# Attention scores of two head pairs as 64x64 products in four quarters of the array, one low part of g on GpSimd, and another order of the token blocks

## The chip, the cores and the metric

One core of one Trainium2 chip. The metric is the time of one execution on the device, in microseconds (us); a kernel's time is the median of its runs. Lower is better.

## The reference

Windowed attention (4 batches, 8 heads, 576 positions, head size 64, window 64), then a gated layer with a rational function, then a product of two linear layers. Cut to what matters:

```
scores = (q @ k.T) / 8                       # only 0 <= i - j < 64 is kept
attn   = softmax(scores)
x      = (attn @ v)  as  2304 tokens x 512
h = x @ w_in                                 # 512 -> 2048
P = a0 + a1*h + a2*h^2 + a3*h^3
Q = 1 + |b0|*|h| + |b1|*h^2
x = (P / (Q + 1e-6)) @ w_out                 # 2048 -> 512
h = (x @ w1) * (x @ w2) @ w3                 # 512 -> 1024 -> 1024
out = h @ w_out2                             # 1024 -> 512
```

The weights arrive as float64; the kernel rebuilds float32 values from the two 32-bit words and keeps them as a high and a low part, so that a product is three products (line 272, `TERMS`).

## The kernel before, in words

The program is not written in the order in which it runs. Each piece of work is declared to a planner (`Plan`, line 66) with the engines it may run on, a cost on each, what it comes after, the buffers it takes and, for some, a due time; the planner simulates all engines, breaks ties with a seeded random number (line 223) and emits every engine's instructions in the order that it found. The order on TensorE is guided by a hand-made sequence (lines 313 to 380): `AT` says at which pair of chunks each attention step stands, `TS`, `TT`, `TO` are costs of scores, transposes and weighted sums.

**Attention.** The 2304 tokens are cut into five blocks (`TOKENS`, line 30), each into two units; a block of 384 has units of 192 tokens (3 windows of 64), a block of 512 has units of 256 (4 windows). A step is one unit and one pair of heads: 40 steps, which come in 20 pairs (`attn`, line 536). A step loads `q`, `k`, `v` (lines 589 to 606), forms for each window the scores of 64 queries against 128 keys (`S_`, line 609), takes the masked minimum on VectorE (`tr`, line 618), the exponential on ScalarE (`e`, line 624), normalizes (`nm`, line 627, on ScalarE, GpSimd or VectorE as the planner chooses), transposes (`T`), copies back (`ac`) and multiplies with `v` (`O`, line 563). The result of a pair is split into a high part (`xh_`, ScalarE) and a low part (`xl_`, VectorE, line 580). In the blocks of 384 that stand first (`THIN`, 16 steps) the two heads of a step are two 64x64 products per window, one in the upper left and one in the lower right quarter of the array. In the other 24 steps a window is one 128x128 product, with the queries of the two heads laid out block-diagonally and padded with zeros by the host (`queries(u, True)`).

**The gated stage.** `chunks` (line 685) takes two chunks of 128 hidden columns at a time, 40 such chunk pairs: `H_` (line 699) into `hp`, the rational function on ScalarE and VectorE (lines 712 to 775), and `D_` (line 777) into four accumulators. Its last step is the low part of `g` (`lo`, line 773), one instruction per chunk, so 80 in all, on VectorE or GpSimd by the planner's choice (line 818). Half of the chunk pairs use another form of the polynomial (`estrin`, line 697). The first three blocks are walked in halves of the hidden columns (`TURNS`, line 307), so their partial sums are stored and added later (`evacuate`, line 831). Between these the weights are rebuilt and split (`conv`, line 431: b0, b1, b2 and lo on VectorE, hi on ScalarE), 72 tiles, with due times (`coming`, lines 887 to 891).

**The rest** is the product of `w3` and the last weight (`w_prod`, line 939) and a scheme with seven products for the two-sided layers (lines 981 to 1256). The change doesn't touch it.

Of the kernel before, what the change touches and what calls it, by code (L numbers as in the profile page):

```python
# [12 lines left out]
F32 = mybir.dt.float32  # L13
# [16 lines left out]
TOKENS = (384, 384, 512, 512, 512)  # L30
# [7 lines left out]
NU = len(US)  # L38
NF = FF // P
# [26 lines left out]
class Plan:  # L66
# [30 lines left out]
    def order(self, rounds=16):  # L97
# [125 lines left out]
        rng = Random(67)  # L223
# [21 lines left out]
def body(ctx: ExitStack, tc: tile.TileContext, qkv, kv0, qk0, w_in, w_out, a, b, w1, w2, w3t, wo2, out):  # L245
# [72 lines left out]
    MM = [{384: TMM, 512: TWM}[t] for t in TOKENS]  # L318
# [4 lines left out]
    TS, TT, TO, TOO = 0.67, 0.33, (0.71, 0.42), 1.9  # L323
# [11 lines left out]
    def then_step(what, i):  # L335
        if 0 <= i < NS:
            then((what, i), {"S": TS, "T": TT, "O": TO[i % 2]}[what] * WIDE(i))
# [11 lines left out]
    for t in range(-2 * NP - 1, NI + 1):  # L349
        scale[0] = 2.9 / (TS + TT + TO[0]) if t < 0 else 1.2 if t < 2 * NP * 2 else 1.0  # L350
# [185 lines left out]
    def attn(pair):  # L536
# [46 lines left out]
        def step(k):  # L583
# [5 lines left out]
            def load(_):  # L589
                x["k"] = ap_.tile([P, KB * W_], F32, tag="k", bufs=rings["k"], name="k")[:, 0:KU]  # L590
                if i < THIN:
                    if k == 0:
                        y["q"] = ap_.tile([P, 2 * UM], F32, tag="q", bufs=rings["q"], name="q")[:, 0:2 * U]
                        nc.sync.dma_start(out=y["q"], in_=qk0[u, p0 // 2])
                    x["q"] = y["q"].rearrange("d (k w n) -> d k w n", k=2, w=NW)[:, k]
                    nc.sync.dma_start(out=x["k"], in_=kv0[u, p, :, 0:KU])
                    return
                q = ap_.tile([P, 2 * UM], F32, tag="q", bufs=rings["q"], name="q")[:, 0:2 * U]
                x["q"] = q.rearrange("d (w n) -> d w n", w=NW)
                nc.sync.dma_start(out=q, in_=qkv[u - THIN // NP, p, :, 0:2 * U])  # L600
                nc.sync.dma_start(out=x["k"], in_=qkv[u - THIN // NP, p, :, 2 * U:2 * U + KU])

            def loadv(_):
                y["v", k] = ap_.tile([P, NWM, P], F32, tag="v", bufs=rings["v"], name="v")[:, 0:NW]
                v = kv0[u, p, :, U + W_:] if i < THIN else qkv[u - THIN // NP, p, :, 2 * U + KB * W_:]
# [3 lines left out]
            def S_(_):  # L609
                x["sp"] = sp = psum.tile([P, NW, P], F32, tag=tags[0], bufs=rings[tags[0]], name="sp")  # L610
                x["sm"] = ap_.tile([P, NWM, P], F32, tag="sm", bufs=rings["sm"], name="sm")[:, 0:NW]
                if k == 0:
                    y["st"] = ap_.tile([P, 8 * NWM], F32, tag="st", bufs=rings["st"], name="st")
# [38 lines left out]
            kb_, vb, qb, mb, sp, tp = ("k", i), ("v", i), ("q", i0 if i < THIN else i), ("sm", i), (tags[0], ("S", i)), (tags[1], ("T", i))  # L652
            thin = i < THIN
            op(("load", i), (("D", (0.48 if k else 1.12) if thin else 1.1 * wide),), load, after=[("load", i0)] if thin and k else (), new=(kb_,) if thin and k else (kb_, qb), uses=(qb,) if thin and k else (), tail=3.0)
            op(("loadv", i), (("D", 0.66 * wide),), loadv, after=(("load", i),), new=(vb,), tail=3.0)
            pe(("S", i), S_, TS * wide, after=[("load", i)] + [("S", i - 1)] * k, new=(sp, mb) if k else (sp, mb, sb), uses=(kb_, qb, sb) if k else (kb_, qb))
            for m in range(NW):
                op(("tr", i, m), (("V", 0.21),), lambda _, m=m: tr(m), after=(("S", i),), uses=(sp, mb, sb))
                op(("e", i, m), (("A", 0.39),), lambda _, m=m: e(m), after=(("tr", i, m),), uses=(mb, sb))
            op(("nm", i), (("A", 0.32 * NW), ("P", 0.97 * wide), ("V", cost(0.065, 0.40))), nm, port=True, after=(("rc", i0),), uses=(sb, mb))  # L660
            moved = i >= MOVED
            if moved:
                op(("mv", i), (("D", 0.66 * wide),), mv, after=[("nm", i)], new=(("tq", i),), uses=(mb,), tail=3.0)
            pe(("T", i), T, 0.068 * NW if moved else TT * wide, after=[("mv", i)] if moved else [("nm", i)], new=(tp,), uses=(("tq", i),) if moved else (mb,))
# [20 lines left out]
    def chunks(c0):  # L685
# [205 lines left out]
    coming = {key: 3.2 * min(n, 12) + 8.5 * max(n - 12, 0) for n, key in enumerate(coming)}  # L891
# [391 lines left out]
def layouts(q, k, v, moe_w_in, moe_w_out, moe_a, moe_b, moe2_w1, moe2_w2, moe2_w3, moe2_w_out):  # L1283
# [26 lines left out]
    def queries(u, apart):  # L1310
# [47 lines left out]
```

## Time and profile before

| what | value |
|---|---|
| median of 3 runs | 804.59 us (804.21 to 805.1) |
| the profiled execution | 805.03 us, of which the span from the first to the last instruction 803.3 us |
| mean granted TensorE clock | 0.995 |
| TensorE busy | 782.0 us, 97% |
| VectorE busy | 729.7 us, 91% |
| ScalarE busy | 542.2 us, 67% |
| GpSimd busy | 50.5 us, 6% |
| moved by DMA | 169.70 MB |

The shares are means over stages: start-up (to about 56 us), gated stage (to about 499 us), then the linear layers. Busy time of TensorE is modelled with pipelined ends, so starts of neighbouring groups say more than durations.

### The profile page before, as it was taken

The page shows a single profiled execution, that of the slowest core. Times are in us where ns is not written, and L with a number is a line of the kernel's source. Part 1 is how long each engine was busy: PE and PEld are TensorE (multiplying, and loading weights), DVE is VectorE, ACT ScalarE, POOL GpSimd, SP SyncE. Part 2 cuts the span into 40 slices and gives each one's busy share as a digit, 9 for nine tenths or more (in the row PEclk, how much of TensorE's full clock was granted, in tenths as well). Part 3 has the DMA queues.
Part 4 walks back from the last instruction along what each step waited for, and adds up shares of the span by engine and source line. Part 5 has one row for each costly group of instructions (what it writes and reads, how often), then busy time and mean ns, then how long its engine had stood idle before and what let it go on. Part 6 is the DMA issues. An engine that isn't in the chain of part 4 may idle for free.

```text
span 803.3 us, 13413 instructions
## 1 busy us (share of the span) xinstructions
PE 782.0 (97%) x4728; PEld 716.3 (89%) x4728; DVE 729.7 (91%) x1361; ACT 542.2 (67%) x1131; POOL 50.5 (6%) x67
## 2 busy tenths in 40 slices
PE   5889999999999999999999999999999999999998
PEld 4679999888899999888888888889999999999998
DVE  6999999999999999999999999999998698847854
ACT  5888998859898988665677772377555447445434
POOL 1112112101100101200100000000000000000000
PEclk9899999999999999999999999999999999999999
DMA  8798884511657755537883365968898676136402
GB/s 292 249 334 305 293 278 157 186 54 65 207 185 282 273 191 203 202 133 236 323 282 143 117 221 183 313 249 292 307 305 282 210 283 195 42 133 222 145 1 78
DMA packets 66403, 169.70 MB, mean 211 GB/s; under 512 B 7456, under 2 KB 24864, under 8 KB 66336
## 3 DMA queue, kind: packets, MB, share of 16 engines
q1 hardware_dynamic: 66336, 168.85, 60.5%
q8 instruction: 37, 0.61, 0.3%
q14 instruction: 30, 0.25, 0.1%
HBM read 123.21 MB, written 41.42 MB: 205 GB/s over the span
## 4 chain that ended last, share of the span: by engine, by line
PE 83%; DVE 12%; DMA 2%; ACT 1%; issue 1%; POOL 0%; SPq 0%; POOLq 0%; DVEq 0%; ACTq 0%
PE acc L781 22%; PE hp L703 20%; PE pb L1093 9%; PE pa L1093 6%; PE pc L1093 6%; PE wp L948 5%; PE pb L1220 5%; PE pc L1220 3%; PE pa L1220 3%; PE sp L616 2%; DVE sm L619 2%; DVE wt L456 1%; DVE wt L453 1%; DVE wc L466 1%; PE op L568 1%; DMA cb<-in_b 1%
## 5 line engine op out<-in xcount | busy, mean ns | idle before, releaser
L703 PE MATMUL hp<-x,wc 128*128 128x512 f32 (+1 forms) x960 | 213.8, 371 | 3.6 <-DVE u L731 3.2
L781 PE MATMUL acc<-g,wc 128*128 128x512 f32 (+1 forms) x960 | 213.1, 370 | 0.0
L703 PEld LDWEIGHTS hp<-x,wc 128*128 128x128 f32 x960 | 173.7, 188 | 27.8 <-DVE u L731 4.2
L781 PEld LDWEIGHTS acc<-g,wc 128*128 128x128 f32 x960 | 173.9, 188 | 22.9 <-issue 0.3
L1093 PE MATMUL pb<-xb,wc 128*128 128x384 f32 x432 | 83.8, 334 | 0.0
L1093 PEld LDWEIGHTS pb<-xb,wc 128*128 128x128 f32 x432 | 75.7, 188 | 0.0
L744 ACT ACTIVATE r<-qa,cq 128x1024 f32<-128x1024 f32 (+1 forms) x40 | 42.8, 1069 | 37.8 <-DVE g L775 21.3
L625 ACT ACTIVATE sm<-sm,st 128x128 f32<-128x128 f32 x144 | 56.1, 395 | 17.3 <-DVE st L619 17.1
L720 ACT ACTIVATE qa<-hp,cb 128x512 f32<-128x512 f32 (+1 forms) x80 | 51.7, 647 | 19.3 <-PE hp L703 19.0
L725 ACT ACTIVATE u<-hp,ca 128x512 f32<-128x512 f32 (+1 forms) x80 | 59.5, 745 | 1.7 <-PE hp L703 1.3
L1093 PE MATMUL pa<-xb,wc 128*128 128x384 f32 x288 | 57.2, 335 | 0.0
L1182 ACT ACTIVATE rt<-prod 128x768 fp32r<-128x768 f32 x42 | 35.6, 847 | 31.9 <-PE pb L1220 13.3
L1093 PE MATMUL pc<-xb,wc 128*128 128x384 f32 x288 | 56.7, 334 | 0.0
L1185 DVE TENSOR_TENSOR rt<-prod,rt 128x768 fp32r<-128x768 f32 x42 | 40.1, 956 | 15.4 <-ACT rt L1182 14.9
L616 PE MATMUL sp<-k,q 64*64 64x128 f32 (+1 forms) x384 | 43.2, 311 | 10.2 <-DMA k<-in_kv 7.2
L463 ACT ACTIVATE wc<-wt 128x512 fp32r<-128x512 f32 x48 | 30.2, 633 | 32.7 <-DVE wt L456 29.0
L1093 PEld LDWEIGHTS pa<-xb,wc 128*128 128x128 f32 x288 | 50.6, 188 | 0.3 <-DMA wc<-kw 0.2
L453 DVE SCALAR_TENSOR_TENSOR wt<-ws,wt 128x512 uint32<-128x512 uint32 x72 | 50.4, 702 | 0.3
L1093 PEld LDWEIGHTS pc<-xb,wc 128*128 128x128 f32 x288 | 50.5, 188 | 0.0
L456 DVE SCALAR_TENSOR_TENSOR wt<-ws,wt 128x512 uint32<-128x512 uint32 x72 | 49.9, 695 | 0.3
L616 PEld LDWEIGHTS sp<-k,q 64*64 64x64 f32 (+1 forms) x384 | 37.9, 182 | 13.7 <-DMA k<-in_kv 4.0
L715 ACT ACTIVATE h<-hp 128x512 f32<-128x512 f32 (+1 forms) x80 | 44.3, 553 | 8.2 <-PE hp L703 7.1
(90 smaller groups left out, 1368.4 us busy)
## 6 DMA issues: line engine op xcount, KB each, us to landing
wc<-kw SPq DMA_DIRECT2D x48, 512.0 KB, 5.4
bs<-kb SPq DMA_DIRECT2D x24, 512.0 KB, 4.5
ws<-in_w_in SPq DMA_DIRECT2D x16, 512.0 KB, 6.1
ws<-in_w_out SPq DMA_DIRECT2D x16, 512.0 KB, 4.2
ws<-in_w SPq DMA_DIRECT2D x16, 512.0 KB, 4.3
kw<-ws SPq DMA_DIRECT2D x16, 512.0 KB, 3.5
ws<-in_w3t SPq DMA_DIRECT2D x16, 512.0 KB, 4.8
wsum<-wsum SPq DMA_DIRECT2D x16, 512.0 KB, 6.1
```

The lines of the kernel that those rows point to most:

```text
L453: stt(out=x["b"], in0=x["st"][:, :, 0], scalar=29, in1=x["b"], op0=ALU.logical_shift_right, op1=ALU.bitwise_or)
L456: stt(out=x["b"], in0=x["st"][:, :, 1], scalar=0xC0000000, in1=x["b"], op0=ALU.bitwise_and, op1=ALU.bitwise_or)
L616: nc.tensor.matmul(sp[h, w, :], x["q"][h, w], x["k"][h, kat[w] * W_:kat[w] * W_ + P], start=True, stop=True)
L625: act(x["sm"][:, m, :], x["sm"][:, m, :], AF.Exp, bias=col(0, k, m), scale=-1.0, accum_out=col(1, k, m))
L703: nc.tensor.matmul(x["hp", m], wf_(win, f0 + m)[:, s_, kk * P:(kk + 1) * P], (xh, xl)[m_][xk][:, kk, :], start=(kk == 0 and i == 0), stop= ...
L715: act(x["h2"][:, m, :], x["hp", m], AF.Square)
L720: act(x["qa"][:, m, :], x["hp", m], AF.Abs, scale=b0)
L725: act(x["u"][:, m, :], x["hp", m], AF.Identity, scale=a3, bias=a2)
L744: act(x["r"], x["qa"], AF.Ln, bias=cq)
L781: nc.tensor.matmul(accs[j, part, n], wf_(wout, f0 + m)[:, s_, n * P:(n + 1) * P], x["g"][:, m_, m, :], start=(first and i == 0), stop=(las ...
L1093: nc.tensor.matmul(x[m], sws[u, n, i0][:, s_, (c0 + k) * P:(c0 + k + 1) * P], t[:, m_, k, :], start=(first and k == 0 and i == 0), stop=(k ...
L1220: nc.tensor.matmul(x[m, n], w[:, s_, (c + n) * P:(c + n + 1) * P], rts[u, b, r][:, m_, k, :], start=(first and r == 0 and k == 0 and i == ...
```

## The change

- **Scores.** All blocks now use 64x64 products. `S_` exists once per pair of steps and issues, for each window, four products: both heads of the first step in the upper left and lower right quarter, both heads of the second step in the other two quarters. The second step's heads thus change places in its score tile, and `O` reads them back from there. The padded queries are gone; one load of `q` serves two steps in all blocks. The scores of a pair now come after both loads of `k`.
- **Low part of g.** In chunk pairs that are not `estrin`, the second chunk's `lo` may run on GpSimd only. `nm` may no longer run on GpSimd.
- **Order.** `TOKENS` is (384, 512, 384, 512, 512), so the second block is now a wide one; `AT`, the seed, costs and the due times of the weights change with it.

```diff
-TOKENS = (384, 384, 512, 512, 512)
+TOKENS = (384, 512, 384, 512, 512)
...
-        rng = Random(67)
+        rng = Random(50)
...
-        AT[((-8, -6, -4, -2), (0, 1, 2, 3), (4, 5, 6, 6), (16, 18, 19, 20), (22, 24, 25, 26))[j][r // 2]].append(i)
+        AT[((-8, -6, -4, -2), (0, 1, 2, 2), (4, 5, 6, 6), (16, 18, 19, 20), (21, 23, 25, 26))[j][r // 2]].append(i)
...
-                for h in (slice(0, 64), slice(64, P)):
-                    nc.tensor.matmul(y["op"][h, k, w * W_:(w + 1) * W_], y["v", k][:, w, h], y["ac", k][:, w, h], start=True, stop=True)
+                for h in range(2):
+                    at = half[h if k == 0 else 1 - h]
+                    nc.tensor.matmul(y["op"][half[h], k, w * W_:(w + 1) * W_], y["v", k][:, w, half[h]], y["ac", k][:, w, at], start=True, stop=True)
...
+        def S_(_):
+            for k in range(2):
+                y["place", k]()
+            y["st"] = ap_.tile([P, 8 * NWM], F32, tag="st", bufs=rings["st"], name="st")
+            for w in range(NW):
+                for k in range(2):
+                    for h in range(2):
+                        to = half[h if k == 0 else 1 - h]
+                        nc.tensor.matmul(y["sp", k][to, w, :], y["q", k][half[h], w], y["k", k][half[h], kat[w] * W_:kat[w] * W_ + P], start=True, stop=True)
...
-                for w in range(NW):
-                    for h in (slice(0, 64), slice(64, P)) if i < THIN else (slice(0, P),):
-                        nc.tensor.matmul(sp[h, w, :], x["q"][h, w], x["k"][h, kat[w] * W_:kat[w] * W_ + P], start=True, stop=True)
...
-            op(("nm", i), (("A", 0.32 * NW), ("P", 0.97 * wide), ("V", cost(0.065, 0.40))), nm, port=True, after=(("rc", i0),), uses=(sb, mb))
+            op(("nm", i), (("A", 0.32 * NW), ("V", cost(0.065, 0.40))), nm, port=True, after=(("rc", i0),), uses=(sb, mb))
...
+            if not estrin and m == 1:
+                engines = (("P", 0.97 * T_ / 384),)
...
-    coming = {key: 3.2 * min(n, 12) + 8.5 * max(n - 12, 0) for n, key in enumerate(coming)}
+    coming = {key: 3.2 * min(n, 10) + 8.5 * max(n - 10, 0) for n, key in enumerate(coming)}
```

Two places in the order of the instructions. On TensorE, the scores of the first wide block (`sp`, line 616 before and 584 now) among the products of the gated stage (`hp` and `acc`), in the kernel before:

```order
L616 MATMUL sp<-k,q 128x128 x8
L781 MATMUL acc_817<-g,wc 128x384 x3
L781 MATMUL acc_808<-g,wc 128x384 x3
L781 MATMUL acc_771<-g,wc 128x384 x3
L703 MATMUL hp<-x,wc 128x384 x12
L781 MATMUL acc_823<-g,wc 128x384 x3
```

and now, where the wide block is the second one and its scores begin ahead of the first `hp`:

```order
L584 MATMUL sp<-k,q 64x128 x16
L649 MATMUL tp<-idr,sm 128x128 x6
L711 MATMUL hp<-x,wc 128x384 x6
L572 MATMUL op<-sm,v 64x64 x12
L711 MATMUL hp<-x,wc 128x384 x15
L649 MATMUL tp<-idr,sm 128x128 x8
L711 MATMUL hp<-x,wc 128x384 x3
L584 MATMUL sp<-k,q 64x128 x16
```

A wide pair of steps was 8 products of the whole array and is 16 products of a quarter; the first wide pair stood behind the `op` of the second block and now stands ahead of the first `hp`.

On GpSimd, the low parts of `g` (line 775 before, 783 now) about the first chunk pairs of 512 tokens, in the kernel before, with the sums' reciprocal preparation (line 558) and normalizations (line 633) among them:

```order
L775 TENSOR_TENSOR g<-u,r 128x384 x2
L558 TENSOR_SCALAR st<-st 128x8
L633 TENSOR_TENSOR sm<-sm,st 128x512
L558 TENSOR_SCALAR st<-st 128x8
L775 TENSOR_TENSOR g<-u,r 128x384 x3
L558 TENSOR_SCALAR st<-st 128x8
L633 TENSOR_TENSOR sm<-sm,st 128x512
L775 TENSOR_TENSOR g<-u,r 128x512 x3
```

and now, from the first chunk pair of 512 tokens on:

```order
L783 TENSOR_TENSOR g<-u,r 128x512
L561 TENSOR_SCALAR st<-st 128x6
L783 TENSOR_TENSOR g<-u,r 128x512 x2
L561 TENSOR_SCALAR st<-st 128x6
L783 TENSOR_TENSOR g<-u,r 128x512 x2
L561 TENSOR_SCALAR st<-st 128x8
L783 TENSOR_TENSOR g<-u,r 128x512
L783 TENSOR_TENSOR g<-u,r 128x384 x5
```

Over the whole list GpSimd has 28 low parts before (17 of 384 columns, 11 of 512) and 33 now (13 and 20), and 7 normalizations before and none now.

## Rows read from the trace of the kernel before

**Rows 1.** The page, busy time of the engines, share of the span and instructions.
```profile
PE 782.0 (97%) x4728; PEld 716.3 (89%) x4728; DVE 729.7 (91%) x1361; ACT 542.2 (67%) x1131; POOL 50.5 (6%) x67
```

**Rows 2.** Busy time in four stretches: PE, PEld, DVE, ACT, POOL (instructions), clock, DMA share, GB/s.
```profile
0.00:56.00 56.00, 38.82 (x397) 31.82 (x397) 48.30 (x151) 41.90 (x133) 9.15 (x24) 0.94 0.86 290
56.00:487.20 431.20, 430.60 (x2602) 381.10 (x2601) 425.59 (x770) 342.10 (x723) 41.32 (x43) 1.00 0.59 207
...
560.00:803.30 243.30, 239.80 (x1383) 239.27 (x1381) 185.03 (x312) 120.09 (x208) 0.00 (x0) 1.00 0.54 185
```

**Rows 3.** TensorE's waits, 0 to 56 us: total, times, longest.
```profile
PE sp L616 <- DMA k<-in_kv: 7.2, 2, 3.6
PE hp L703 <- DVE u L731: 2.6, 1, 2.6
```

**Rows 4.** TensorE's waits, 56 us to the end, all of them.
```profile
PE hp L703 <- DVE u L731: 0.6, 1, 0.6
```

**Rows 5.** VectorE's waits, 56 to 487 us, the longest.
```profile
DVE st L561 <- POOL st L558: 1.2, 1, 1.2
DVE u L728 <- ACT u L725: 0.9, 1, 0.9
```

**Rows 6.** The chain of waits where the gated stage ends.
```profile
488.47 5.44 PE wp L948 x24
493.91 5.44 PE acc L781 x24
```

**Rows 7.** TensorE in order of time: start, duration, what; a group overlaps the next.
```profile
50.88 1.62 PE L568 MATMUL op<-sm,v 128*64 128x64 f32 x48
52.43 0.79 PE L703 MATMUL hp<-x,wc 128*128 128x384 f32 x3
...
60.28 2.24 PE L703 MATMUL hp<-x,wc 128*128 128x384 f32 x12
62.36 0.68 PE L781 MATMUL acc<-g,wc 128*128 128x384 f32 x3
...
63.46 1.31 PE L781 MATMUL acc<-g,wc 128*128 128x384 f32 x6
64.69 1.53 PE L616 MATMUL sp<-k,q 64*64 64x128 f32 x24
66.15 2.36 PE L781 MATMUL acc<-g,wc 128*128 128x384 f32 x12
...
75.41 1.84 PE L781 MATMUL acc<-g,wc 128*128 128x384 f32 x9
77.08 2.00 PE L616 MATMUL sp<-k,q 128*128 128x128 f32 x16
78.83 1.84 PE L781 MATMUL acc<-g,wc 128*128 128x384 f32 x9
```

**Rows 8.** Groups of VectorE by line and shape: count, busy us, mean ns of one.
```profile
L775 DVE TENSOR_TENSOR g<-u,r 128x512 fp32r<-128x512 f32 x37 | 25.0, 707 | 0.0
...
L775 DVE TENSOR_TENSOR g<-u,r 128x384 fp32r<-128x384 f32 x15 | 8.1, 573 | 0.1
...
L855 DVE TENSOR_TENSOR xe<-xe,acc 128x384 f32<-128x384 f32 x8 | 4.3, 548 | 0.1
...
L855 DVE TENSOR_TENSOR xe<-xe,acc 128x512 f32<-128x512 f32 x4 | 2.6, 680 | 0.0
...
L861 DVE COPY xe<-acc 128x512 f32<-128x512 f32 x1 | 0.7, 695 | 0.0
```

**Rows 9.** The same of ScalarE, the normalization.
```profile
L631 ACT ACTIVATE sm<-sm,st 128x128 f32<-128x128 f32 x69 | 22.1, 393 | 0.7 <-DVE st L561 0.6
```

**Rows 10.** Busy time in one stretch of the start, columns as in group 2.
```profile
40.00:60.00 20.00, 16.07 (x161) 14.16 (x160) 19.64 (x55) 17.62 (x51) 2.33 (x3) 1.00 0.97 337
```

**Rows 11.** All engines in order of time, the first scores.
```profile
7.13 0.43 DVE L450 TENSOR_SCALAR wt<-ws 128x512 uint32<-128x512 uint32 x1 [1.70 <-DMA ws<-in_w_in]
...
8.69 2.82 PE L616 MATMUL sp<-k,q 64*64 64x128 f32 x24 [3.60 <-DMA k<-in_kv]
```

More of the change, by code (lines that the diff above doesn't have):

```diff
@@ L38 @@
 NU = len(US)
+THINU = NU
 NF = FF // P
@@ L244, in body @@
 @with_exitstack
-def body(ctx: ExitStack, tc: tile.TileContext, qkv, kv0, qk0, w_in, w_out, a, b, w1, w2, w3t, wo2, out):
+def body(ctx: ExitStack, tc: tile.TileContext, kv0, qk0, w_in, w_out, a, b, w1, w2, w3t, wo2, out):
     nc = tc.nc
@@ L315, in body @@
         j, r = divmod(i, 2 * NP)
-        AT[((-8, -6, -4, -2), (0, 1, 2, 3), (4, 5, 6, 6), (16, 18, 19, 20), (22, 24, 25, 26))[j][r // 2]].append(i)
+        AT[((-8, -6, -4, -2), (0, 1, 2, 2), (4, 5, 6, 6), (16, 18, 19, 20), (21, 23, 25, 26))[j][r // 2]].append(i)
     TMM, TWM = 0.1735, 0.227
-    MM = [{384: TMM, 512: TWM}[t] for t in TOKENS]
+    MM = [{256: 0.12, 384: TMM, 512: TWM}[t] for t in TOKENS]
     THIN = qk0.shape[0] * NP
@@ L335, in then_step @@
     def then_step(what, i):
-        if 0 <= i < NS:
+        if 0 <= i < NS and (what != "S" or i % 2 == 0):
             then((what, i), {"S": TS, "T": TT, "O": TO[i % 2]}[what] * WIDE(i))
@@ L549, in attn @@
         y = units.setdefault(u, [{} for _ in range(NP // 2)])[p0 // 2]
+        half = (slice(0, 64), slice(64, P))
         def rows(f):
@@ L590, in load @@
                 x["k"] = ap_.tile([P, KB * W_], F32, tag="k", bufs=rings["k"], name="k")[:, 0:KU]
[L591 to L601, printed above, removed]
+                if k == 0:
+                    y["q"] = ap_.tile([P, 2 * UM], F32, tag="q", bufs=rings["q"], name="q")[:, 0:2 * U]
+                    nc.sync.dma_start(out=y["q"].rearrange("d (k n) -> d k n", k=2), in_=qk0[u, p0 // 2].rearrange("d (k n) -> d k n", k=2)[:, :, 0:U])
@@ L603, in loadv, with place @@
+                y["q", k] = y["q"].rearrange("d (k w n) -> d k w n", k=2, w=NW)[:, k]
+                nc.sync.dma_start(out=x["k"], in_=kv0[u, p, :, 0:KU])
+                y["k", k] = x["k"]
             def loadv(_):
                 y["v", k] = ap_.tile([P, NWM, P], F32, tag="v", bufs=rings["v"], name="v")[:, 0:NW]
-                v = kv0[u, p, :, U + W_:] if i < THIN else qkv[u - THIN // NP, p, :, 2 * U + KB * W_:]
+                v = kv0[u, p, :, KU:KU + NW * P]
                 nc.sync.dma_start(out=y["v", k], in_=v.rearrange("r (w d) -> r w d", w=NW))
-            def S_(_):
-                x["sp"] = sp = psum.tile([P, NW, P], F32, tag=tags[0], bufs=rings[tags[0]], name="sp")
+            def place():
+                y["sp", k] = x["sp"] = psum.tile([P, NW, P], F32, tag=tags[0], bufs=rings[tags[0]], name="sp")
@@ L650, in ac @@
                 act(y["ac", k], x["tp"], cp)
-            kb_, vb, qb, mb, sp, tp = ("k", i), ("v", i), ("q", i0 if i < THIN else i), ("sm", i), (tags[0], ("S", i)), (tags[1], ("T", i))
-            thin = i < THIN
-            op(("load", i), (("D", (0.48 if k else 1.12) if thin else 1.1 * wide),), load, after=[("load", i0)] if thin and k else (), new=(kb_,) if thin and k else (kb_, qb), uses=(qb,) if thin and k else (), tail=3.0)
+            kb_, vb, qb, mb, sp, tp = ("k", i), ("v", i), ("q", i0), ("sm", i), (tags[0], ("S", i)), (tags[1], ("T", i))
@@ L655, in step @@
+            thin = True
+            op(("load", i), (("D", (0.48 if k else 1.12) * wide),), load, after=[("load", i0)] if thin and k else (), new=(kb_,) if thin and k else (kb_, qb), uses=(qb,) if thin and k else (), tail=3.0)
             op(("loadv", i), (("D", 0.66 * wide),), loadv, after=(("load", i),), new=(vb,), tail=3.0)
-            pe(("S", i), S_, TS * wide, after=[("load", i)] + [("S", i - 1)] * k, new=(sp, mb) if k else (sp, mb, sb), uses=(kb_, qb, sb) if k else (kb_, qb))
+            if k == 0:
+                sp1, mb1 = (f"acc{(i + 1) % 2}" if early else "at", ("S", i + 1)), ("sm", i + 1)
+                pe(("S", i), S_, TS * wide, after=[("load", i), ("load", i + 1)], new=(sp, mb, sb, sp1, mb1), uses=(kb_, qb, ("k", i + 1)))
@@ L661, in step @@
             moved = i >= MOVED
             if moved:
-                op(("mv", i), (("D", 0.66 * wide),), mv, after=[("nm", i)], new=(("tq", i),), uses=(mb,), tail=3.0)
-            pe(("T", i), T, 0.068 * NW if moved else TT * wide, after=[("mv", i)] if moved else [("nm", i)], new=(tp,), uses=(("tq", i),) if moved else (mb,))
+                op(("mv", i), (("D", 0.66 * wide),), mv, after=[("nm", i)], new=(("tq", i),), uses=(mb,), tail=2.0)
+            pe(("T", i), T, 0.075 * NW if moved else TT * wide, after=[("mv", i)] if moved else [("nm", i)], new=(tp,), uses=(("tq", i),) if moved else (mb,))
@@ L1322, in queries @@
         return out.reshape(NP, P, -1)
-    thin = range(4)
-    qk0 = np.stack([queries(u, False) for u in thin])
+    thin = range(THINU)
+    pad = lambda x: np.concatenate([x, np.zeros((NP, P, KB * W_ + NWM * P - x.shape[2]), x.dtype)], axis=2)
+    qk0 = np.stack([pad(queries(u, False))[:, :, :UM] for u in thin])
     return {
-        "qkv": np.stack([np.concatenate([queries(u, True), keys(u, KB), values(u)], axis=2) for u in range(4, NU)]),
-        "kv0": np.stack([np.concatenate([keys(u, len(blocks(u)[0])), values(u)], axis=2) for u in thin]),
-        "qk0": qk0.reshape(4, NP // 2, 2, P, -1).transpose(0, 1, 3, 2, 4).reshape(4, NP // 2, P, -1),
+        "kv0": np.stack([pad(np.concatenate([keys(u, len(blocks(u)[0])), values(u)], axis=2)) for u in thin]),
+        "qk0": qk0.reshape(THINU, NP // 2, 2, P, -1).transpose(0, 1, 3, 2, 4).reshape(THINU, NP // 2, P, -1),
         "w_in": cols(moe_w_in, NF),
```

9 lines of the change are left out of this document (4 added, 5 removed).

## The prediction

> **What bounds the kernel now.** The page first: TensorE is busy 97% of the span, VectorE 91%, ScalarE 67%, GpSimd 6% [rows 1]. A share over the whole span doesn't say who waits for whom, so the next view is the busy time by stretch [rows 2]. From 56 to 487.2 us, the gated stage with most of the attention in it, TensorE is busy for 430.6 of 431.2 us and VectorE for 425.6: both engines are full at once. From 560 us on TensorE is full and VectorE has 58 us to spare. The list of waits agrees: TensorE's waits lie in the first 56 us, where it is idle for 17.2 us in all [rows 2], 7.2 of it for keys [rows 3]; after that one wait of 0.6 us is all that the list has [rows 4]. So time taken off TensorE in the gated stage is worth its full size only where VectorE can follow, and that is the question of this case. Where the stage ends, TensorE has 5.44 us of the weight product ahead of the last 24 products into the accumulators [rows 6]: work that doesn't need `g` covers the last chain on VectorE.
>
> **Scores.** The timeline shows starts of groups [rows 7]. A wide pair of steps (16 passes over 128 columns of the whole array; float32 takes two passes a product) starts at 77.08 and the next product at 78.83: 1.75 us, 0.109 a pass. The nine products ahead of it take 1.67 us, against 1.56 at the 0.173 of the twelve `hp` that start at 60.28: 0.11 us on entry. Together 1.86. A pair of a block of 384, in two quarters, has 24 passes from 64.69 to 66.15: 1.46 us, 0.061 a pass, so two run at a time (12 x 0.109 = 1.31, and 0.15 at the end). Six products ahead of it take 1.23 us, not 1.04: 0.19 on entry. Together 1.65.
>
> Four at a time is not in the trace; it is bounded by rows. The weighted sums use two column halves over all rows: 48 passes of 64 columns from 50.88 to 52.43, 0.032 each, against half of 0.109: two column halves run at once. The 384 scores show two row halves at once. If both hold together, a 384 pair costs 0.19 + 6 x 0.109 + 0.15 = 0.99 (0.66 less) and a wide pair 0.19 + 8 x 0.109 + 0.15 = 1.21 (0.65 less). If still only two run, a 384 pair stays at 1.65 and a wide pair is 0.19 + 16 x 0.109 + 0.15 = 2.08 (0.22 more). I take four: the pieces that it is made of are both seen, and entry and exit are already paid in the 384 row. The four pairs of the first block lie where TensorE idles anyway, so 16 pairs count: **10.4 us off TensorE** (20 pairs: 13.1).
>
> The two heads of a step write the two partition halves of one PSUM bank, and their 24 passes take half of 24 x 0.109 [rows 7]. The Trainium skill, page "TensorEngine Tiling (Array Packing)", section "Restrictions and Gotchas", says that different row tiles cannot access one PSUM bank at the same time. For halves that differ in partitions the rows here speak against it. By that rule the two heads of a step would exclude each other and at most two products would run: the second bound above, a rival below.
>
> **Low part of g and the rest of VectorE.** In the order of the whole program GpSimd has 33 low parts instead of 28, and they are wider. VectorE has 28 of 512 instead of 37, and 19 of 384 instead of 15: 9 x 0.707 - 4 x 0.573 = 4.1 us less [rows 8]. The other order of blocks makes evacuation dearer: three more copies of accumulators on VectorE (of ScalarE's 19 there are 16 left), one at 0.695 and two that I put at the 0.548 of an addition of that size, and four additions at 0.680 instead of 0.548: 2.3 us more [rows 8]. The normalizations on VectorE stay 14. Sum: **1.8 us less VectorE**. The seven normalizations that leave GpSimd go to ScalarE: 94 windows there instead of 69, 25 x 0.393 = 9.8 us more [rows 9], beside other work on an engine that is busy for 342 of 431 us [rows 2]. I cost it at nothing; if the cover is gone, the exponentials behind it are late, and with them the transposes. GpSimd has the time for five more.
>
> Can VectorE put work off instead? Of 72 weight tiles, 60 have their third conversion step ahead of the fortieth and last update of `qa` (line 764) in the order before, and 60 now. So no: it has the same work up to there, less 1.8 us.
>
> **Order and loads.** The second block now has 32 windows instead of 24, all wanted before the fifth chunk pair; the third has 24 instead of 32. Work moves ahead and none is added. Its loads move ahead too: eight steps with a third more `v` and `q` and longer keys, 1.05 MB by the shapes at the least, where the DMA engines are busy 97% at 337 GB/s [rows 10]. Later loads shrink, since one `q` of 256 KB serves two wide steps (12 loads fewer); no wait in [rows 4] is a DMA, so that is worth nothing. The first scores now wait for both key tiles, until 8.69 instead of 3.55 us [rows 11]; VectorE starts its first conversion at 7.13, and the little that it did before (one masked minimum) it does later: at most 0.4 us, hidden.
>
> **The sum.** From 56 to 487.2 us VectorE idles for 431.2 - 425.6 = 5.6 us [rows 2]; its longest waits there are for GpSimd's sums and ScalarE's `u` [rows 5], not for TensorE directly. With 1.8 us less work the stage can end at most 5.6 + 1.8 = 7.4 us earlier, less than TensorE's 10.4. A faster TensorE feeds ScalarE and through it VectorE, so part of the idle time goes; what waits for ScalarE, which gets 9.8 us more, stays. I take half: 2.8 + 1.8 = 4.6 us. The other 5.8 us of TensorE's gain turn into waits for VectorE. Behind 487 us nothing changes. 805.0 - 4.6 = 800.4 on the profiled execution, which stands 0.4 above the median of the runs: **800.0 us**, with 797.2 (all 7.4) to 802.8 (the 1.8 alone) for this case.
>
> **Rivals.**
> 1. TensorE alone decides. For: it has no waits after 56 us, and the planner may place VectorE's conversions so that none is late. Against: VectorE's 5.6 us of idle time. 804.6 - 10.4 = 794.2, with the first block too 791.5.
> 2. No gain: VectorE's idle time stays, because ScalarE's longer queue holds it, and grows by about as much as the 1.8 us. 803.0 to 806.2, likeliest 804.6.
> 3. The start gets longer. In 20 to 60 us the wide second block's 1.05 MB come on a full DMA; at 300 GB/s that is 3.5 us by which keys, values or weights land later, and VectorE idles. It decides if the loads of weights, whose due times the change also stretches, don't give way. VectorE then has 3.5 us more idle time against 1.8 less work: 804.6 + 1.7 = 806.3, and more if the scores' later start adds to it.
> 4. The change doesn't do what it says: two products at a time only. 12 wide pairs at 0.22 more: 804.6 + 2.6 = 807.2. Against it: the two rows of halves above.
>
> **How the numbers follow.** Forecast 0.50, rival 1 0.21, rival 2 0.15, rival 3 0.08, rival 4 0.06. A measurement of this kernel tells about 0.2% (1.6 us) from no change, so faster is under 803.0: the forecast and rival 1, 0.71. Rival 2 is within: 0.15. Rivals 3 and 4 are above 806.2: 0.14. The range leaves out these two and the lowest end of rival 1: 793.0 to 805.5.
>
> **What would show it.** Right: a wide pair of scores near 1.2 us from start to start; new waits of TensorE for VectorE after 56 us, some 5 us in all; VectorE's idle time up to its fortieth update of `qa` down by about 3 us; the stage's end some 5 us earlier and the rest after it as long as before. Wrong: scores of a wide pair at 2 us (rival 4), TensorE without waits and the end 10 us earlier (rival 1), or TensorE and VectorE idle for loads before 80 us (rival 3).

## The result, and the profile after

The changed kernel takes **811.83 us** (median of 4 runs, 811.58 to 815.98), the kernel before in the same comparison 804.4 us, which is 7.4 us less. The ratio of the means is 1.0103, 95% interval 1.0070 to 1.0137. It is 1% slower; the forecast was 800.0 us, with 793.0 to 805.5 as its range.

The profiled execution spans 810.0 us. Page of the changed kernel, busy time, to be held against [rows 1]:

```profile
PE 776.6 (96%) x4920; PEld 699.6 (86%) x4920; DVE 732.3 (90%) x1359; ACT 545.5 (67%) x1153; POOL 72.0 (9%) x65
```

The same stretches as [rows 2], of the changed kernel:

```profile
0.00:56.00 56.00, 34.33 (x343) 27.18 (x343) 47.36 (x159) 40.47 (x138) 4.10 (x18) 0.91 0.87 289
56.00:487.20 431.20, 423.30 (x2821) 364.69 (x2821) 421.27 (x751) 342.88 (x737) 67.93 (x47) 1.00 0.57 199
```

TensorE now idles 7.9 us in the second stretch, not 0.6, and VectorE 9.9 us, not 5.6. GpSimd is busy for 67.93 us there, not 41.32.

The chain of waits of the changed kernel where the gated stage ends, against [rows 6]:

```profile
497.05 1.21 DVE u L776
498.26 0.68 DVE wt L451 x2
498.93 0.60 DVE wt L454
499.53 0.61 DVE g L783
500.14 0.04 issue
500.19 5.75 PE acc L789 x24
505.94 9.07 PE wp L958 x40
```

The last 24 products into the accumulators end at 505.94 instead of 499.35 us, 6.6 us later, and the span is 6.7 us longer: all of the loss lies in the gated stage, the linear layers after it take as long as before. The chain is VectorE's there; before, it was TensorE's.

For the rest of the text one number stands for the stage: the start of the fortieth and last update of `qa` (line 764 before, 772 after) on VectorE, split into VectorE's busy and idle time ahead of it (the spans of its instructions in the trace, overlaps counted once). Before: 487.1 us = 473.9 busy + 13.2 idle. After: **495.3 = 476.8 + 18.5**. At the 26th update the two kernels stand level, 335.7 and 335.1 us; the loss comes after it.

The scores themselves do what was forecast. TensorE of the changed kernel in order of time, a wide pair twice, against [rows 7]:

```profile
63.28 1.10 PE L584 MATMUL sp<-k,q 64*64 64x128 f32 x32
64.31 1.31 PE L711 MATMUL hp<-x,wc 128*128 128x384 f32 x6
...
69.20 1.10 PE L584 MATMUL sp<-k,q 64*64 64x128 f32 x32
70.23 0.79 PE L789 MATMUL acc<-g,wc 128*128 128x384 f32 x3
```

From start to start it is 1.03 us for 32 passes, where 16 passes of the whole array took 1.75. A pair of a block of 384 takes 0.82 for 1.46:

```profile
99.42 0.89 PE L584 MATMUL sp<-k,q 64*64 64x128 f32 x24
100.24 1.65 PE L711 MATMUL hp<-x,wc 128*128 128x512 f32 x6
```

All scores together take 24.7 us from start to start, 37.9 before. TensorE's busy time on the page falls by 5.4 us only (776.6 for 782.0): the 1152 products of 512 columns in `hp` and `acc` take 5.3 us more by their starts, though their median stays at 0.227 us. What holds single ones up by about 0.1 us is not shown.

What is new is on GpSimd. Its low parts, by line and shape, in the changed kernel:

```profile
L783 POOL TENSOR_TENSOR g<-u,r 128x512 fp32r<-128x512 f32 x20 | 39.1, 1967 | 132.2 <-DVE u L778 53.8 <-DVE u L776 43.7 <-ACT qa L728 16.2
L783 POOL TENSOR_TENSOR g<-u,r 128x384 fp32r<-128x384 f32 x13 | 16.8, 1307 | 67.5 <-DVE u L778 28.2 <-DVE u L776 22.8 <-PE acc L789 8.1
```

and in the kernel before:

```profile
L775 POOL TENSOR_TENSOR g<-u,r 128x384 fp32r<-128x384 f32 x17 | 19.4, 1159 | 65.7 <-DVE u L770 30.9 <-ACT u L725 13.5 <-ACT sm L650 10.8
L775 POOL TENSOR_TENSOR g<-u,r 128x512 fp32r<-128x512 f32 x11 | 14.9, 1370 | 139.4 <-DVE u L768 59.6 <-PE hp L703 41.7 <-DVE u L770 38.0
```

The same instruction over 512 columns takes 1.97 us instead of 1.37 in the mean. Around the longest of them, all engines in order of time (in brackets the idle time before and who ended it):

```profile
409.08 1.27 DVE L748 SCALAR_TENSOR_TENSOR qa<-h,cab,qa 128x1024 f32<-128x1024 f32 x1
409.33 6.59 POOL L783 TENSOR_TENSOR g<-u,r 128x512 fp32r<-128x512 f32 x1 [8.42 <-ACT ws L464]
410.28 0.68 DVE L783 TENSOR_TENSOR g<-u,r 128x512 fp32r<-128x512 f32 x1
410.88 0.68 DVE L467 TENSOR_TENSOR ws<-wt,ws 128x512 fp32r<-128x512 f32 x1
...
411.49 1.21 DVE L758 TENSOR_TENSOR u<-u,h 128x1024 f32<-128x1024 f32 x1
...
412.62 0.41 DVE L451 TENSOR_SCALAR wt<-ws 128x512 uint32<-128x512 uint32 x1
412.96 1.21 DVE L761 TENSOR_TENSOR u<-u,bl 128x1024 f32<-128x1024 f32 x1
414.09 0.68 DVE L454 SCALAR_TENSOR_TENSOR wt<-ws,wt 128x512 uint32<-128x512 uint32 x1
...
415.96 1.15 ACT L752 ACTIVATE r<-qa,cq 128x1024 f32<-128x1024 f32 x1 [6.12 <-POOL g L783]
417.14 1.06 ACT L755 ACTIVATE r<-r 128x1024 f32<-128x1024 f32 x1
...
418.24 1.23 DVE L767 TENSOR_TENSOR g<-u,r 128x1024 fp32r<-128x1024 f32 x1 [3.46 <-ACT r L755]
```

How long a low part takes goes with what VectorE does beside it, not with VectorE being busy. The low part at 409.33 us starts inside a `qa` sum (line 748). That sum and what follows it read two tiles of SBUF, the memory that holds the low part's `u` and `r` too; only line 451, the first step of a conversion, reads one. The last of them ends at 414.77 us, and the low part 1.15 us later. The 61 low parts on GpSimd in the two traces fall in two groups:

- Those that start beside an instruction of VectorE that reads a result of TensorE in PSUM or a single tile of SBUF, or beside none, take 1.00 to 1.02 us at 384 columns and 1.27 to 1.30 at 512, though VectorE is busy nearly all the while: 23 of 28 before, 15 of 33 now.
- Those that start where VectorE is in, or just entering, an instruction with both inputs in SBUF take 1.29 to 2.79 us and once 6.59: 5 of 28 before, **18 of 33** now. Against the short times (1.01 and 1.29) GpSimd's low parts take 17 us more in all, 3 before.

The planner has a rule for this: `ports` (line 93 before, 94 now) never lets a GpSimd operation overlap one of VectorE that is marked `port`. But only the order of its plan is kept on the chip, not the times, and 15 of the 18 start beside a marked one. The other three start beside steps of a conversion (lines 454 and 457) that are not marked.

A low part reads `r`, of which there is one buffer. ScalarE can't write the next `r` until GpSimd is done, and VectorE needs that `r` for the next `g`. ScalarE's waits, 56 us to the fortieth update, changed kernel:

```profile
ACT r L752 <- DVE g L783: 21.3, 9, 4.0
ACT r L752 <- POOL g L783: 13.6, 5, 6.1
```

For GpSimd's low parts (line 775) ScalarE waited 0.8 us, once, in the kernel before. VectorE's longest waits in the same stretch, changed kernel, against [rows 5]:

```profile
DVE g L767 <- ACT r L755: 4.2, 3, 3.5
DVE u L736 <- ACT h L723: 1.5, 3, 0.6
DVE sm L625 <- PE sp L584: 1.4, 4, 0.6
```

And TensorE's, 56 us to the stage's end, against [rows 4]:

```profile
PE acc L789 <- DVE g L783: 2.9, 3, 1.9
PE hp L711 <- DVE u L739: 2.8, 4, 1.3
```

### The profile page after: what moved, and what is told of

Same layout as the page of the kernel before. It is cut to its first block, busy times and chain, and to the rows that moved or that the text cites. A ratio compares the mean times of both kernels' runs of the same rounds, so it can differ in the third digit from the quotient of the medians.

```text
span 810.0 us, 13831 instructions
## 1 busy us (share of the span) xinstructions
PE 776.6 (96%) x4920; PEld 699.6 (86%) x4920; DVE 732.3 (90%) x1359; ACT 545.5 (67%) x1153; POOL 72.0 (9%) x65
## 4 chain that ended last, share of the span: by engine, by line
PE 59%; DVE 28%; ACT 7%; issue 3%; DMA 2%; POOL 0%; SPq 0%; DVEq 0%; ACTq 0%; POOLq 0%
PE acc L789 11%; PE hp L711 10%; PE pb L1103 8%; PE pa L1103 6%; PE pc L1103 6%; PE wp L958 5%; PE pb L1230 5%; PE pc L1230 3%; PE pa L1230 3%; DVE qa L748 3%; DVE qa L772 3%; DVE wt L454 2%; DVE wt L457 2%; DVE g L783 2%; ACT sm L631 2%
## 5 line engine op out<-in xcount | busy, mean ns | idle before, releaser
L783 POOL TENSOR_TENSOR g<-u,r 128x512 fp32r<-128x512 f32 (+1 forms) x33 | 56.0, 1707 | 199.7 <-DVE u L778 82.0
L1103 PE MATMUL pc<-xb,wc 128*128 128x384 f32 x288 | 56.5, 334 | 0.0
L748 DVE SCALAR_TENSOR_TENSOR qa<-h,cab,qa 128x1024 f32<-128x1024 f32 (+1 forms) x40 | 50.1, 1252 | 0.3 <-ACT h L723 0.3
L457 DVE SCALAR_TENSOR_TENSOR wt<-ws,wt 128x512 uint32<-128x512 uint32 x72 | 49.1, 682 | 0.2
L454 DVE SCALAR_TENSOR_TENSOR wt<-ws,wt 128x512 uint32<-128x512 uint32 x72 | 49.0, 682 | 0.2
```

What stands on the lines that cost most here:

```text
L454: stt(out=x["b"], in0=x["st"][:, :, 0], scalar=29, in1=x["b"], op0=ALU.logical_shift_right, op1=ALU.bitwise_or)
L457: stt(out=x["b"], in0=x["st"][:, :, 1], scalar=0xC0000000, in1=x["b"], op0=ALU.bitwise_and, op1=ALU.bitwise_or)
L748: stt(out=x["qa"], in0=x["h2"], scalar=b1, in1=x["qa"], op0=MUL, op1=ADD)
L783: engine[e].tensor_tensor(out=x["g"][:, 1, m], in0=x["u"][:, m], in1=x["r"][:, m], op=MUL)
L1103: nc.tensor.matmul(x[m], sws[u, n, i0][:, s_, (c0 + k) * P:(c0 + k + 1) * P], t[:, m_, k, :], start=(first and k == 0 and i == 0), stop=(k ...
```

## Experiments

The trace left two suspects, and a third that has to be kept in mind because the planner makes a new order for whatever is changed: **(1)** the low parts that GpSimd must take; **(2)** the scores of two steps, now one piece of work that needs both keys and both score buffers at once; **(3)** the new plan as such. All medians and ratios (of the means) to the kernel before, with the stage's number:

| run | us | ratio, 95% interval | 40th update = VectorE busy + idle |
|---|---|---|---|
| before | 804.0 to 805.2 | | 487.1 = 473.9 + 13.2 |
| the change | 811.83 | 1.0103 (1.0070 to 1.0137) | 495.3 = 476.8 + 18.5 |
| e1_lo_on_vector | 812.18 | 1.0099 (1.0082 to 1.0115) | 495.1 = 481.7 + 13.4 |
| e2_lo_free | 808.30 | 1.0053 (1.0038 to 1.0068) | 491.1 = 476.9 + 14.2 |
| e3_before_forced | 811.70 | 1.0097 (1.0080 to 1.0114) | 490.7 = 478.5 + 12.2 |
| p2_after_zero | 806.01 | 1.0010 (0.9996 to 1.0024) | 488.9 = 471.5 + 17.4 |
| p3_before_lo_v | 814.58 | 1.0119 (1.0093 to 1.0144) | 497.0 = 484.6 + 12.4 |
| e4_quarters_only | 813.87 | 1.0124 (1.0109 to 1.0139) | 496.0 = 481.9 + 14.1 |
| e5_quarters_same | 823.05 | 1.0216 (1.0195 to 1.0237) | 506.0 = 477.1 + 28.9 |
| p1_quarters_in_plan | 819.51 | 1.0191 (1.0158 to 1.0223) | 501.4 = 473.9 + 27.5 |
| p4_pair_in_plan | 815.74 | 1.0130 (1.0096 to 1.0164) | 495.8 = 474.7 + 21.1 |
| e6_lo_free_act | 811.51 | 1.0086 (1.0069 to 1.0102) | 492.5 = 471.9 + 20.6 |
| e7_before_act | 812.42 | 1.0097 (1.0082 to 1.0112) | 492.7 = 466.3 + 26.3 |
| e8_quarters_act | 816.81 | 1.0149 (1.0134 to 1.0164) | 498.6 = 475.6 + 23.1 |
| s1_before_seed50 | 807.45 | 1.0013 (0.9978 to 1.0049) | 488.9 = 476.9 + 12.0 |
| s2_before_seed3 | 809.13 | 1.0062 (1.0036 to 1.0087) | 490.6 = 475.7 + 14.9 |
| s3_after_seed67 | 814.94 | 1.0132 (1.0103 to 1.0161) | 496.4 = 481.1 + 15.3 |
| s4_after_seed3 | 808.88 | 1.0063 (1.0044 to 1.0082) | 489.4 = 476.8 + 12.6 |
| b1_late_lo_free | 817.34 | 1.0152 (1.0135 to 1.0169) | 490.0 = 471.1 + 19.0 |
| b2_late_before | 814.30 | 1.0116 (1.0100 to 1.0131) | 490.5 = 475.6 + 14.9 |

### GpSimd's low parts

**e1_lo_on_vector**: the plan of the changed kernel, with the 20 low parts that must run on GpSimd issued on VectorE.

```diff
-op(("lo", c0 + m), engines, lambda e, m=m: lo(m, e), ...
+op(("lo", c0 + m), engines, lambda e, m=m: lo(m, "V" if not estrin and m == 1 else e), ...
```

> The changed kernel with its plan kept; only the 20 low parts of g that it forces onto GpSimd are issued on VectorE, at the same place of the order. Theory 1 (the forced low parts lose: beside a busy VectorE one takes up to 6.59 us instead of about 1.3, and the single buffer r and with it ScalarE's logarithm wait for it): 803 to 808 us, the wait of 3.46 us near 415 us gone. Theory 2 (the other order of the blocks and the fuller start lose): VectorE has 20 x 0.65 = 13 us more work, so 812 to 822 us.

812.18 us, as the changed kernel: the lower end of theory 2's range, but with 4.9 us more work on VectorE and not 13, and with 5.1 us less idle time. Taken from VectorE in this way, the 20 low parts give back in waits all that they save.

**p2_after_zero**: the plan of the changed kernel; in place of those 20 products GpSimd writes zeros.

```diff
 def lo(m, e):
+    if not estrin and m == 1:
+        nc.gpsimd.memset(x["g"][:, 1, 1].bitcast(F32), 0.0)
+        return
```

> The changed kernel with its plan held; in place of the 20 forced low parts GpSimd writes zeros, so these low parts are left out of the result. If GpSimd's product beside VectorE is what loses (it reads two inputs while VectorE reads two): 801 to 806 us, and VectorE's Q back from 1.25 to 1.17 us mean. If only the list of VectorE is too long: 809 to 812 us.

806.01 us, 5.8 less than the changed kernel and at the end of the first range; the mean of the `qa` sums falls to 1.22 us, not to 1.17. VectorE issues the same instructions in both, and yet its busy time falls by 5.3 us. Its own low parts in the changed kernel:

```profile
L783 DVE TENSOR_TENSOR g<-u,r 128x512 fp32r<-128x512 f32 x28 | 19.7, 721 | 0.1
...
L783 DVE TENSOR_TENSOR g<-u,r 128x384 fp32r<-128x384 f32 x19 | 12.3, 676 | 0.0
```

and in p2, where the line is 786:

```profile
L786 DVE TENSOR_TENSOR g<-u,r 128x512 fp32r<-128x512 f32 x28 | 18.6, 681 | 0.1
...
L786 DVE TENSOR_TENSOR g<-u,r 128x384 fp32r<-128x384 f32 x19 | 9.9, 548 | 0.0
```

So it costs both: GpSimd's low part takes longer, and so do VectorE's instructions with two inputs in SBUF. The Trainium skill, page "SBUF — State Buffer", section "Who interferes with whom", says that a VectorE instruction with two inputs in SBUF contends with a GpSimd instruction that reads SBUF, and not with one that only writes it; the zeros only write, and the two groups agree: 676 ns against 548.

**e2_lo_free**: the change without the rule that forces them; the planner chose 19 low parts for GpSimd and not 33.

```diff
-            if not estrin and m == 1:
-                engines = (("P", 0.97 * T_ / 384),)
```

> The changed kernel with the planner free to put every low part of g on VectorE or GpSimd, as before; planned anew. Theory 1: 798 to 804 us. Theory 2: within 2 us of the changed kernel's 811.8.

808.30 us, between the two ranges: 3.5 us less than the change, and that is idle time of VectorE (14.2 for 18.5) at equal work. Where the planner may choose, 5 of the 19 low parts start beside a two-input instruction of VectorE. But this is a new order too, and the seeds below move the changed kernel by more than 3.5 us.

**e3_before_forced**: the same two lines added to the kernel before.

> The kernel before with the rule on low parts alone (second chunk of the pairs that are not estrin: GpSimd only); planned anew. Theory 1: 808 to 814 us. Theory 2: 803 to 806 us.

811.70 us, 7.7 more, as theory 1 expected. In the profiled execution (810.59 us) the last products into the accumulators end 4.3 us later (503.68 us), and GpSimd's low parts are 39 and take 55.3 us. Of the 39, 15 start beside a two-input instruction (5 of 28 without the rule). With the new order that comes with it, the rule costs the kernel before as much as the whole change.

**p3_before_lo_v**: the plan of the kernel before, its 28 low parts of GpSimd issued on VectorE.

```diff
-op(("lo", c0 + m), engines, lambda e, m=m: lo(m, e), ...
+op(("lo", c0 + m), engines, lambda e, m=m: lo(m, "V"), ...
```

> The kernel before with its plan held, and its 28 low parts on GpSimd issued on VectorE: 28 x about 0.62 = 17 us more work there. If GpSimd relieves VectorE by as much as it takes over: 815 to 822 us. If, as in e1, the two hold each other up and little is won by GpSimd: 805 to 812 us.

814.58 us, between the two ranges. The counterpart of e1: where the planner put them, GpSimd's low parts save VectorE 10.7 us of work, cost it 0.8 us of idle time, and are worth 10 us. There 5 of 28 started beside a two-input instruction, in the changed kernel 18 of 33. So it isn't GpSimd as such that loses but a low part that must go there wherever it falls.

### The scores as quarters

**e4_quarters_only**: the quarters, with everything else as before (the order of blocks, `AT`, the seed, the due times, the rules for `lo` and `nm`); the planner makes a new order.

```diff
-TOKENS = (384, 512, 384, 512, 512)
+TOKENS = (384, 384, 512, 512, 512)
-        rng = Random(50)
+        rng = Random(67)
...
```

> The scores in four quarters alone, with the block order, the places of the attention steps, the seed, the weights' due times and the engines of the low part and of the normalization as in the kernel before. The forecast's reasoning (TensorE 10 us less, VectorE lets through a part): 797 to 803 us. Theory 2 agrees. If the quarters themselves lose: over 806 us.

813.87 us: the quarters alone, in the order that the planner makes of them, are slower than before and no faster than the whole change (814.94 with the same seed, s3 below). Idle time is up by 0.9 us only, VectorE's work by 8.0: in the new order it gets 59 low parts and 5 copies of accumulators ahead of the fortieth update instead of 50 and 1.

**e5_quarters_same**: e4 with the engine of each low part, normalization and copy fixed as the plan of before had it.

```diff
+        engines = fixed(key, engines)
```

> The scores in four quarters alone, as in e4, but every low part, normalization and evacuation is held on the engine that the plan of the kernel before gave it (28 low parts on GpSimd, 50 on VectorE ahead of its fortieth update of qa). Theory V (what VectorE has to do ahead of that update sets the time, and the new plan of e4 gave it 8 us more): 803 to 806 us. Theory Q (the quarters lose by themselves): 810 to 814 us, as e4.

823.05 us, above both ranges: with the division of work of before VectorE's work is nearly back (477.1), and the stage is worse still, 28.9 us idle. So bringing VectorE's work back was not enough. The run doesn't separate the quarters from GpSimd, though: its 28 low parts there are forced ones again, in a new order, and 15 of them start beside a two-input instruction.

**p1_quarters_in_plan**: the pieces of work stay as they were declared, so the plan of before holds for every other instruction; at the place of a pair's first step all four quarters are issued, after both loads.

```diff
+                if k:
+                    return
+                y["load", 1](None)
+                for kk in range(2):
+                    y["place", kk]()
...
+                for w in range(NW):
+                    for kk in range(2):
+                        for h in range(2):
```

> The kernel before with its plan held: every engine's list is as before, only the scores of a pair are issued together, at the first step's place, as 64x64 products in four quarters (one load of q for two steps). Theory P (the rules are worth what the forecast said, and new plans lose it): 797 to 803 us. Theory W (in one plan TensorE's gain turns into waits for the full VectorE, and scores that wait for both steps' keys and buffers add some): 804 to 810 us.

819.51 us, above both ranges. VectorE's work is that of before to 0.02 us, and all of the 14.2 us are idle time. VectorE's waits for scores in 0 to 510 us, in p1:

```profile
DVE sm L631 <- PE sp L628: 13.5, 11, 5.9
```

and in the kernel before:

```profile
DVE sm L619 <- PE sp L616: 2.3, 3, 1.6
```

**p4_pair_in_plan**: the same without quarters: both steps' scores at the first step's place, as the products of the kernel before, step by step (the lines are shown against p1).

```diff
-                for w in range(NW):
-                    for kk in range(2):
-                        for h in range(2):
+                for kk in range(2):
+                    for w in range(NW):
+                        for h in (slice(0, 64), slice(64, P)) if i < THIN else (slice(0, P),):
```

> The plan of the kernel before is held, and both steps of a pair issue their scores together at the place of the first step, but as the products of the kernel before, no quarters. If it is the coupling of the two steps that costs (both keys and both score buffers have to be there), the time is near that of the same plan with quarters, 815 to 822 us, and the quarters themselves are worth little. If the quarters themselves lose, it is near the kernel before, 804 to 808 us.

815.74 us, as expected of the coupling, so 10.6 us are lost without any quarter. The quarters on top of it gain nothing, though TensorE has less to do: in the profiled executions the first update of `qa` comes at 51.2 us in p4 and 55.0 in p1, since the quarters take the windows of both steps in turn, so that the first masked minimum waits for both keys (it starts at 9.45 us in p1, at 5.30 in p4); from the first to the fortieth update it is 444.6 us and 446.3. In the kernel before that is 436.1 us. Where the rest of p4's time goes, 180 to 350 us, TensorE's only wait:

```profile
PE op L568 <- DVE x L581: 5.9, 2, 3.0
```

In the kernel before TensorE had no wait at all in that stretch. A plan that was made for single steps is the worst case for pairs, so these sizes are not those of the change itself; that the coupling has a price, and that TensorE's gain doesn't pay it, is what the two runs show.

### ScalarE only

**e6_lo_free_act**, **e7_before_act**, **e8_quarters_act**: e2, before and e4 with normalizations on ScalarE only, and of the evacuations only the additions on VectorE.

```diff
-(("A", 0.32 * NW), ("V", cost(0.065, 0.40))), nm
+(("A", 0.32 * NW),), nm
...
```

> e2 with all normalizations and all plain evacuation copies on ScalarE: VectorE loses 15 and 6 instructions ahead of its fortieth update of qa, 12 us. Theory V: 796 to 800 us, until TensorE or ScalarE is the bound. Theory 1 (the low parts on GpSimd are what loses): within 2 us of e2's 808.3.

> The kernel before with the same two rules (normalizations and evacuation copies on ScalarE): VectorE loses 10 us of work there. TensorE has no waits in the kernel before after 56 us, so nothing can be won but in the start: 802 to 805 us by theory V with two bounds. If VectorE alone were the bound of the kernel before: 795 to 798 us.

> e4 with the same two rules: 21 instructions fewer (13 us) and 9 low parts more (5.6 us) on VectorE ahead of its fortieth update of qa. Theory V: 805 to 808 us. Theory Q: 810 us or more.

VectorE's work falls by 5.0, 7.6 and 6.3 us and its idle time rises by 6.4, 13.1 and 9.0. All three are slower than without the edit, e6 and e7 above all that was expected. In the three new orders that this made, work moved from VectorE to a less busy ScalarE came back as waits.

### The plan as such

**s1_before_seed50, s2_before_seed3, s3_after_seed67, s4_after_seed3**: nothing but the seed of the planner's random numbers (the lines are those of s2).

```diff
-        rng = Random(67)
+        rng = Random(3)
```

> The kernel before with the changed kernel's seed; nothing else. Theory P (the plan decides: the kernel before stands on a seed whose plan fits well, and any new plan, whatever its rules, costs 4 to 18 us, as the eight runs so far): 807 to 816 us. Theory R (the rules that were changed decide): 803 to 806 us.

> The kernel before with a third seed. Theory P: 807 to 816 us. Theory R: 803 to 806 us.

> The changed kernel with the seed of the kernel before. Theory P: somewhere from 806 to 822 us, not near 811.8 by rule. Theory R: 810.5 to 813 us.

> The changed kernel with a third seed. Theory P: 806 to 822 us. Theory R: 810.5 to 813 us.

All four lie in theory P's ranges, though s1's interval takes in no change; s2 to s4 have 3, 2 and 5 runs. Over the seeds 67, 50 and 3 the kernel before takes 804.6, 807.5 and 809.1 us, the changed one 814.9, 811.8 and 808.9. The seed moves the one by 4.5 us, the other by 6.1, nearly as much as the change did. With the seed that each was given the change costs 7 us; on the mean of three, 811.9 against 807.1, it costs 4.8; with seed 67 it costs 10, with seed 3 nothing. Three seeds are too few to call the 4.8 us the price of the rules. The changed kernel's three plans differ in how the low parts fall: with seeds 67, 50 and 3 ScalarE waits 17.9, 13.6 and 6.8 us for those on GpSimd, and 17 of 30, 18 of 33 and 12 of 36 start beside a two-input instruction of VectorE. That fits the order of their times; it doesn't prove that the times come from it.

### Towards a better version

**b1_late_lo_free** and **b2_late_before**: e2 and before, with the conversions of `w1` and `w2` due later, so that VectorE has fewer of them in the gated stage.

```diff
-conv("w1", w1c, n, w1[n], None, pre=215.0 + 32.0 * n, kept=0)
+conv("w1", w1c, n, w1[n], None, pre=215.0 + 42.0 * n, kept=0)
...
```

> The change with the planner free to place the low parts, and with the conversions of w1 and w2 due later: 57 conversions and 49 low parts (59 and 59 without) stand on VectorE ahead of the 40th update of qa, some 10 us less of VectorE's work. If VectorE's list sets the end of the stage, 799 to 806 us; if the plan and the coupling of the steps set it, 806 to 812 us.

> The kernel before with the same later due times of the conversions of w1 and w2: 58 conversions, 45 low parts and 9 evacuation copies on VectorE ahead of the 40th update of qa. If VectorE's list sets the end of the stage, 797 to 803 us; if a new plan alone costs some microseconds, 803 to 810 us.

817.34 and 814.30 us: both expectations missed. b1's fortieth update comes 5.3 us earlier than the changed kernel's, but then one low part on VectorE is late and TensorE stands still for 4.71 us. TensorE in b1, and the busy time there, columns as in [rows 2]:

```profile
497.66 8.23 PE L789 MATMUL acc<-g,wc 128*128 128x512 f32 x24 [4.71 <-DVE g L783]
```

```profile
492.00:497.00 5.00, 0.96 (x5) 0.46 (x3) 5.00 (x9) 1.23 (x2) 0.00 (x0) 0.92 0.56 188
497.00:502.00 5.00, 4.34 (x10) 3.47 (x11) 3.44 (x8) 0.64 (x1) 0.00 (x0) 0.50 0.33 119
```

After the pause the granted clock is 0.50, the level of 1.2 GHz, and the last 24 products take 8.23 us instead of 5.75. So the stage ends at 505.74 us, level with the changed kernel, and what was put off is missed behind it: from 540 to 600 us TensorE has 314 products where the changed kernel has 342, with waits for `wf` and `wc`. In b2 VectorE's work grew instead, by 1.7 us (9 copies of accumulators for one). No version was found that beats the kernel before.

## Why the prediction was wrong, step by step

- **The quarters**: right. A wide pair takes 1.03 us from start to start for the forecast 1.02 (8 x 0.109 + 0.15); four run at a time. Rival 4 and the rule of the Trainium skill behind it (page "TensorEngine Tiling (Array Packing)", section "Restrictions and Gotchas", on row tiles and one PSUM bank) are out for this use: two heads in the two partition halves of one bank did not exclude each other.
- **"10.4 us off TensorE"**: for the scores themselves the size was right (13.2 us over all 20 pairs, forecast 13.1); the page's busy time fell by 5.4 us only, and what it was worth was nothing. The prediction had VectorE limit the gain, but took it for granted that shorter scores come no later. It costed the coupling of two steps only at the first pair ("at most 0.4 us, hidden"). In p1 and p4 the coupling costs 10.6 us and more in a plan that doesn't allow for it, and the quarters gain nothing back.
- **"1.8 us less VectorE"**: wrong, it was 2.9 us more. The evacuation's part was right (2.2 us for 2.3). The low parts' part was 4.1 us less, and is 1.1: [rows 8] had 25.0 + 8.1 us, now 19.7 + 12.3, since a low part of 384 takes 676 ns instead of 573 beside GpSimd. The `qa` sums of line 740 (748 now), unmoved, take 2.3 us more over the forty.
- **"GpSimd has the time for five more"**: the step that failed first, and with it the 4.1 us that moving the low parts was to save at no price. A share of 6% [rows 1] said nothing about what a low part meets there. Now 18 of 33 start beside a two-input instruction of VectorE, where 5 of 28 did, and since `r` has one buffer a late low part holds ScalarE (13.6 us of waits for 0.8) and then VectorE. Where the plan is held, the 20 forced low parts take as long on GpSimd as on VectorE (e1), and without them the kernel is 5.8 us faster (p2).
- **"I take half"** of the 5.6 us of idle time as gain: wrong in sign. From the first to the fortieth update idle time rose from 5.6 to 9.9 us. One wait behind the 6.59 us on GpSimd is 3.5 of it, but that isn't its price: p2, without that wait, idles 9.7 us there with 5.3 us less work, so a VectorE that is relieved soon meets the next wait.
- **Normalizations on ScalarE at nothing**: not tested by itself. e6 to e8 take more of them away from VectorE and are slower.
- **Rival 3** had the right sign with another mechanism: VectorE's first update came 5.5 us later (56.5 for 51.1), but the kernels were level again by the 26th. Rival 2's reason, idle time that grows behind ScalarE, is the nearest to what happened; it was priced too low.

How the 7.4 us divide is shown in part: p2 bounds what the products of the 20 forced low parts cost in this plan at 5.8 us; e2's 3.5 us without the rule holds for another order. The rest belongs to quarters, order and plan together, and these don't add up: e4, with less changed, is no faster than the change, and the seeds move both kernels by nearly as much. No run changes the order of the blocks, the due times or the normalization's engines alone. How that rest divides stays open.

## What to carry to other kernels

Where two engines are full at once, time taken off one may be worth nothing, and an edit that makes two pieces of work wait for each other has a price even where it saves instructions: cost the coupling for every pair, not for the first. Work handed to an idle engine has to be costed by which instructions of the busy one it falls beside and by whose buffer it holds meanwhile; a rule that forces it there takes from the planner the choice of a place where it costs little. Before a difference of 1% is put down to a rule of a planner, change its seed: here that alone moved the time by up to 6 us.

## What was not expected of the hardware

- The same GpSimd product over 512 columns took from 1.28 to 6.59 us in the changed kernel. A busy VectorE by itself cost it nothing: at 123.16 us it took 1.30 beside a VectorE that worked all the time, but on `hp` and scores in PSUM. In the 6.59 us VectorE was busy for 5.44, all but 0.4 with two inputs in SBUF. The busy time in the two stretches:

```profile
123.16:124.46 1.30, 1.30 (x6) 0.89 (x6) 1.30 (x12) 1.30 (x5) 1.30 (x2) 1.00 0.99 348
409.33:415.92 6.59, 6.59 (x31) 5.46 (x30) 5.44 (x7) 0.51 (x1) 6.59 (x1) 1.00 0.99 305
```

- It works both ways: in p2, without the 20 products, VectorE's unaltered instructions took 5.3 us less in all. One case of the changed kernel, where both products end up longer than alone (1.01 us on GpSimd, 0.55 on VectorE):

```profile
92.84 0.64 DVE L467 TENSOR_TENSOR wc<-wt,wc 128x512 fp32r<-128x512 f32 x1
92.99 1.36 POOL L783 TENSOR_TENSOR g<-u,r 128x384 fp32r<-128x384 f32 x1 [1.04 <-DVE st L564]
93.41 1.36 DVE L783 TENSOR_TENSOR g<-u,r 128x384 fp32r<-128x384 f32 x1
```

- Four 64x64 quarters of the array in float32 ran 32 passes over 128 columns in 1.03 us, 0.032 us a pass; a pass of the whole array took 0.109. Four at a time would be 0.027; the 0.16 us more in all is near the 0.15 that the two quarters showed at the end [rows 7].
